# A two-stage token-mixing kernel on one core: its hand-merged generators against recorded tasks that a list scheduler puts in order, with r loaded six tokens to a partition

## Chip, cores, metric

The kernel runs on one core of one Trainium2 chip. The metric is the device time of one execution in microseconds; a median of several runs is given. The profile is that of one execution; for the kernel before it was one of 218.0 us, which is not among the first three below and is 4 us faster than their median. The span, which the profile page states, is about 2 us shorter than the time of the same execution.

The engines are called as the profile calls them: PE is TensorE (PEld its weight loads), DVE is VectorE, ACT is ScalarE, POOL is GpSimd, SP is SyncE, which here only issues transfers.

## The reference

```python
# r, k, v: (4, 8, 768, 48) = batch, head, token, dim; w, u: (8, 48)
for t in range(S):                       # stage 1: a linear attention with decay w
    kt, vt, rt = k[:, :, t], v[:, :, t], r[:, :, t]
    cur   = einsum('bhd,bhe->bhde', u * kt, vt)
    y[:, :, t] = einsum('bhd,bhde->bhe', rt, state + cur)
    state = w * state + einsum('bhd,bhe->bhde', kt, vt)
x = y.transpose(0, 2, 1, 3).reshape(B, S, 384)
theta  = x @ w_theta                     # stage 2: mixing over tokens and channels
zr, zi = x * cos(theta), x * sin(theta)
uu = x + w_tok_r @ zr + w_tok_i @ zi     # 768 x 768 weights, over tokens
out = uu + relu(uu @ w_ch)
```

Both kernels do stage 1 in blocks of 128 tokens. r and k are scaled by powers of w, transposed on PE, evicted to SBUF, multiplied (scores), masked, and applied to v; a running state Y carries what lies before the block. Call stage 1 and the computation of theta, cos and sin of one batch its *front*, and the rest its *mixing*.

## The kernel before

Each stage is a Python generator, and a merge function draws from mixing(b) and front(b+1) in turn. Within what is drawn, the framework's own scheduler orders the instructions. PSUM is cut into three pools of 2, 3 and 3 banks. The pieces that matter here are these (cuts are marked):

```python
loads = ctx.enter_context(tc.tile_pool(name="loads", bufs=7))
for src, nm, eng in ((k, "k_f", nc.scalar), (r, "r_f", nc.sync), (v, "v_f", nc.sync)):
    ts = [loads.tile([C, H, D], F32, name=nm) for c in range(CPH)]
    for c in range(CPH):                         # 128 tokens x 8 heads x 192 bytes each
        eng.dma_start(out=ts[c],
            in_=src[b, :, t0 + c*C : t0 + (c+1)*C, :].transpose([1, 0, 2]))
# ... cut: front, for one block of 128 tokens
p = transposes([Rw ... x4] + [Kw ... x4])        # 8 transposes into one PSUM tile
nc.scalar.activation(RKT.rearrange("p a h t -> p (a h) t"), p, Act.Copy)   # 1024 wide, contiguous
# ... cut: scores, mask, outputs; after the whole of Y:
nc.scalar.activation(Sb[q, :, hp, hi*D:(hi+1)*D], Y[q, :, hp, :], Act.Copy,
                     scale=wC[q, hp:hp+1])       # 8 of these for a batch
# ... cut
merge((mixing(b), 18), (front(b + 1), 21))
```

## Time and profile before

The median of the first three runs is 222.4 us (221.7 to 224.5).

| view | reading |
|---|---|
| span | 216.3 us |
| busy PE / DVE / ACT / POOL | 151.3 / 127.8 / 110.6 / 75.6 us |
| last zr multiply of batch 0, 1, 2, 3 ends at | 61.5, 115.3, 154.9, 193.1 us |
| DMA queues | 81051 packets, 58.0% of 16 engines' span (sum of the queue shares) |

The third row is read from the timeline of DVE: the zr multiply is the last step of a batch's front, so its end is a milestone, and the differences between milestones are the time of one batch. First come lines of the profile page: busy time, then the busy tenths of 40 equal slices of the span (a slice is 5.4 us; PEclk is the clock that TensorE was granted).

```profile
PE 151.3 (70%) x1561; PEld 100.9 (47%) x1561; DVE 127.8 (59%) x268; ACT 110.6 (51%) x194; POOL 75.6 (35%) x89
...
PE   0004696049459689789897987787997778797782
...
ACT  0076363366984468865674351748555173841101
...
PEclk9999999999985589999999999999999999999997
DMA  5999999999999969278502001020200102020122
```

No engine is full as a whole, and the DMA engines are nearly full for the first third. The timeline shows how the kernel starts (start and length in us, engine, line, operation):

```profile
3.22 8.63 ACTq L74 DMA_DIRECT2D k_f<-in_k_dram  x5
...
11.88 1.28 ACT L110 ACT_TABLE_LOAD   x1 [11.88 <-DMA k_f<-in_k_dram]
...
15.86 0.60 ACT L114 ACTIVATE wpinv<-lw_f,niota_p 128x384 f32<-128x384 f32 x1
```

ACT is busy issuing loads until 11.9 us and only then computes the powers of w. In a steady batch (a window of 38.3 us; each engine's busy time and its number of instructions, then clock, DMA share, GB/s) PE works 31.1 us:

```profile
core 0: us, PE busy (x) PEld busy (x) DVE busy (x) ACT busy (x) POOL busy (x), PEclk, DMA share, GB/s
116.70:155.00 38.30, 31.13 (x371) 20.58 (x369) 26.97 (x59) 20.93 (x35) 15.66 (x17) 1.00 0.09 32
```

Finally the costliest ACT group and one of the state scalings (count, busy us, mean ns of one, idle time before it).

```profile
L203 ACT ACTIVATE RKT<-tp 128x1024 bf16<-128x1024 bf16 x24 | 24.1, 1023 | 16.6 <-PE tp L154 14.0 <-DMA wsq_f<-in_moe_w_theta_dram 1.5 <-PE mm L237 1.0
...
L254 ACT ACTIVATE Sblk_172<-Y,wC 64x240 bf16<-64x240 f32 x16 | 7.9, 492 | 4.6 <-DVE Y L247 4.4
```

### The profile page before, as it was taken

Reading aid. Unit: us, or ns where it says so; the run is one execution under the profiler, and the core shown is the slowest. Engines: PE = TensorE matmul, PEld = TensorE weight load, DVE = VectorE, ACT = ScalarE, POOL = GpSimd, SP = SyncE. Lnnn points to the kernel's source line nnn. Section 1 sums busy time; section 2 is a strip of 40 time slices with the busy share of each in tenths; the row PEclk is TensorE's granted clock in tenths of the full one; section 3 lists DMA queues with packets and bytes.
Section 4 is the critical chain, followed back from the end, with each engine's and each line's share of the span. In section 5 each row is a group of like instructions: output and inputs, shape, how many; then the busy total and the mean of one; then the engine's idle time right before and its main releaser. Section 6 shows DMA issues by size and latency. Waiting matters only on the chain.

```text
span 216.3 us, 4058 instructions
## 1 busy us (share of the span) xinstructions
PE 151.3 (70%) x1561; PEld 100.9 (47%) x1561; DVE 127.8 (59%) x268; ACT 110.6 (51%) x194; POOL 75.6 (35%) x89
## 2 busy tenths in 40 slices
PE   0004696049459689789897987787997778797782
PEld 0003475036237466665554555564554556444450
DVE  1009988525676785366656899445698944643231
ACT  0076363366984468865674351748555173841101
POOL 8309338241771733102344481306313120630000
PEclk9999999999985589999999999999999999999997
DMA  5999999999999969278502001020200102020122
GB/s 120 188 187 263 269 211 200 238 190 176 191 198 226 257 168 282 74 146 184 144 2 77 0 20 57 3 73 0 76 0 14 62 0 76 2 73 17 59 73 73
DMA packets 81051, 25.23 MB, mean 117 GB/s; under 512 B 75528, under 2 KB 79496, under 8 KB 81032
## 3 DMA queue, kind: packets, MB, share of 16 engines
q1 hardware_dynamic: 54784, 17.31, 39.1%
q10 hardware_dynamic: 26248, 7.67, 18.4%
q8 instruction: 12, 0.20, 0.4%
q14 instruction: 7, 0.06, 0.1%
HBM read 20.25 MB, written 4.72 MB: 115 GB/s over the span
## 4 chain that ended last, share of the span: by engine, by line
PE 43%; ACT 24%; DMA 16%; DVE 12%; issue 3%; ACTq 1%; SPq 0%
PE mm L322 9%; PE mm L319 9%; DMA k_f<-in_k_dram 7%; PE tp L154 6%; DMA v_f<-in_v_dram 6%; ACT RKT L203 5%; PE mm L331 5%; PE at L212 3%; PE mm L297 3%; ACT uT L286 3%; ACT Sblk_172 L254 3%; PE tp L173 3%; DMA r_f<-in_r_dram 3%; DVE prodT L207 3%; ACT Sblk_170 L254 3%
## 5 line engine op out<-in xcount | busy, mean ns | idle before, releaser
L261 POOL TENSOR_TENSOR ydiag<-dg,vb 128x384 bf16<-128x384 f32 x24 | 21.3, 903 | 42.6 <-DVE x_n L277 23.9
L303 POOL TENSOR_TENSOR zi<-x_n,sinv 128x384 bf16<-128x384 bf16 x24 | 22.4, 945 | 38.4 <-ACT sinv L301 36.0
L203 ACT ACTIVATE RKT<-tp 128x1024 bf16<-128x1024 bf16 x24 | 24.1, 1023 | 16.6 <-PE tp L154 14.0
L218 DVE TENSOR_TENSOR mAT<-at,mask_131 128x512 bf16<-128x512 f32 x48 | 31.1, 682 | 2.1 <-PE at L212 1.8
L319 PE MATMUL mm<-zr,WrT 128*128 128x384 bf16 x144 | 29.1, 326 | 2.9 <-DVE Y L247 1.7
L322 PE MATMUL mm<-zi,WiT 128*128 128x384 bf16 x144 | 28.0, 326 | 0.0
L304 DVE TENSOR_TENSOR zr<-x_n,cosv 128x384 bf16<-128x384 bf16 x24 | 17.5, 733 | 13.0 <-ACT cosv L302 13.0
L324 DVE TENSOR_TENSOR u_n<-x_n,mm 128x384 bf16<-128x384 bf16 x24 | 13.3, 552 | 19.0 <-PE mm L322 18.8
L196 POOL TENSOR_TENSOR Rw_158<-r_f,wpow 128x384 bf16<-128x384 f32 x12 | 12.9, 1081 | 24.6 <-PE tp L154 9.0
L212 PE MATMUL at<-RKT 64*128 64x128 bf16 x192 | 16.0, 250 | 7.0 <-ACT RKT L203 6.5
L334 DVE SCALAR_TENSOR_TENSOR fin<-mm,u_n 128x384 f32<-128x384 f32 x24 | 13.1, 554 | 12.7 <-PE mm L331 12.7
L331 PE MATMUL mm<-Wch,uT 128*128 128x384 bf16 x72 | 15.2, 327 | 7.5 <-ACT uT L286 7.5
L286 ACT ACTIVATE uT<-tp 128x768 bf16<-128x768 bf16 x12 | 9.8, 815 | 18.2 <-PE tp L154 18.0
L322 PEld LDWEIGHTS <-WiT 128*128 128x128 bf16 x144 | 13.9, 98 | 10.1 <-issue 1.2
L297 PE MATMUL mm<-Wth,xT 128*128 128x384 bf16 x72 | 15.5, 344 | 4.4 <-ACT xT L286 4.0
L319 PEld LDWEIGHTS <-WrT 128*128 128x128 bf16 x144 | 13.5, 97 | 10.4 <-DVE Y L247 2.1
L277 DVE TENSOR_TENSOR x_n<-mm,ydiag 128x384 bf16<-128x384 f32 x24 | 12.8, 551 | 8.3 <-PE mm L273 8.2
L207 DVE TENSOR_TENSOR prodT<-RKT 128x512 bf16<-128x512 bf16 x24 | 13.5, 564 | 6.8 <-ACT RKT L203 6.7
L196 POOL TENSOR_TENSOR Rw_162<-r_f,wpow 128x384 bf16<-128x384 f32 x12 | 12.8, 1074 | 11.2 <-DMA r_f<-in_r_dram 5.1
L286 ACT ACTIVATE xT<-tp 128x768 bf16<-128x768 bf16 x12 | 9.5, 818 | 13.3 <-PE tp L154 13.3
L301 ACT ACTIVATE sinv<-mm 128x384 bf16<-128x384 f32 x24 | 11.8, 493 | 8.7 <-PE mm L297 8.4
L173 PE MATMUL tp<-ident_f,wn 128*128 128x128 f32 x72 | 14.8, 326 | 0.8 <-DMA wn<-in_moe_w_tok_r_dram 0.5
(84 smaller groups left out, 253.7 us busy)
## 6 DMA issues: line engine op xcount, KB each, us to landing
k_f<-in_k_dram ACTq DMA_DIRECT2D x24, 192.0 KB, 4.8
r_f<-in_r_dram SPq DMA_DIRECT2D x24, 192.0 KB, 6.3
v_f<-in_v_dram SPq DMA_DIRECT2D x24, 192.0 KB, 5.2
out_dram<-fin SPq DMA_DIRECT2D x24, 192.0 KB, 1.9
wn<-in_moe_w_tok_i_dram ACTq DMA_DIRECT2D x6, 384.0 KB, 4.8
wn<-in_moe_w_tok_r_dram SPq DMA_DIRECT2D x6, 384.0 KB, 4.6
wsq_f<-in_moe_w_theta_dram ACTq DMA_DIRECT2D x1, 576.0 KB, 7.9
wsq_f<-in_moe_w_ch_dram SPq DMA_DIRECT2D x1, 576.0 KB, 7.7
```

The source lines that it names most:

```text
L173: nc.tensor.matmul(p[:, j, :], wn[:, 3 * sg + j, :], ident_f, is_transpose=True, start=(j == 0), stop=(j == 2))
L196: nc.gpsimd.tensor_mul(Rw[:, c, :, :D], r_f[c], wpow)
L203: nc.scalar.activation(RKT.rearrange("p a h t -> p (a h) t"), p, Act.Copy)
L212: nc.tensor.matmul(ats[hi][:, hp, :], RKT[q, 1, hp, :], RKT[q, 0, hp, :], start=(hp == 0), stop=(hp == HP - 1))
L218: nc.vector.tensor_mul(mAT[:, hi], ats[hi], mask_bc)
L261: nc.gpsimd.tensor_mul(ydiag, dataclasses.replace(dgc, ap=list(dgc.ap) + [[0, D]]), vb[:, cc])
L286: nc.scalar.activation(dst.rearrange("p t d c -> p (t d) c"), p, Act.Copy)
L297: nc.tensor.matmul(th_p, xT[:, to % 2, dk, :], Wth[:, dk, :], start=(dk == 0), stop=(dk == ND - 1))
L303: nc.gpsimd.tensor_mul(zi[:, to, :], x_n[:, to, :], sinv)
L319: nc.tensor.matmul(y_p, WrT[:, so, to * C:(to + 1) * C], zr[:, so, :], start=(so == 0), stop=False)
L322: nc.tensor.matmul(y_p, WiT[:, so, to * C:(to + 1) * C], zi[:, so, :], start=False, stop=(so == NCH - 1))
L331: nc.tensor.matmul(f_p, uT[:, to % 2, dk, :], Wch[:, dk, :], start=(dk == 0), stop=(dk == ND - 1))
```

## The change

The intent is a better order on every in-order engine, and cheaper loads. All work is recorded first as tasks, each with an engine, an estimated duration in ns, what it reads and writes, and a priority. A list scheduler then plays the tasks forward in time, at each moment starting the ready task of best priority on each free engine, and hands out eight PSUM banks from one pool. The instructions are emitted in that order.

```diff
+class Plan:
+    def add(self, eng, ns, fn, rd=(), wr=(), prio=0.0, lat=60.0, acq=(), use=(), mode=None): ...
+    def order(self):                      # cut to its core
+        for e in waiting:
+            while free_at[e] <= now:
+                best = # the ready task of lowest (prio, seq) whose PSUM banks are free
+                free_at[e] = now + best.ns
+                best.end = now + best.ns + best.lat
+                out.append(best)
+
+    def act_ns(n, psum=True):
+        return n / 1.2 + (60 if psum else 95)
+
+    def load_r(b):                        # six tokens, 1152 bytes, to a partition
+        P.add(SP, 3200, lambda: nc.sync.dma_start(
+            out=t, in_=r[b].rearrange("h (p n) d -> p h (n d)", n=NCH)), ...)
+
+    def flip6(dst, blocks, tok, prio, rd, wr):
+        P.add(PE, 55 * n, go, ..., acq=[tok])            # n transposes into a bank
+        P.add(ACT, act_ns(n * C), lambda: nc.scalar.activation(
+            dst, bank16(tok)[:, :n * C].rearrange("p (a c) -> p a c", a=n), Act.Copy), ...)
+
+        # r: token 6p + n stands in partition p, so its transposes come out n by n,
+        # and the eviction puts them back in the order of tokens
+        flip6(RT[:, hp].rearrange("q (p n) -> q n p", n=NCH),
+              [Rw[:, n, 2*hp:2*hp+2, :] for n in range(NCH)], ...)
...
-    merge((front(0, *cur), 21))
+    front(0, 0); token_weights(20); square(moe_w_ch, Wch, "Wch", 40)
+    for b in range(B):
+        if b + 1 < B: front(b + 1, 100 * (b + 1))
+        mixing(b, 100 * b + 150)
+    for t in P.order(): t.fn()
```

Smaller parts that come with it: all large loads are issued by SP, the state is scaled on POOL block by block instead of on ACT at the end, cos goes back to PSUM and is read from there, and k, v and the diagonal term are handled two blocks at a time.

## The prediction

> **What bounds it now.** Span 216.3 us; median of three runs 222.4. No engine is full (busy: PE 151.3, DVE 127.8, ACT 110.6, POOL 75.6 us); the limit differs by stage.
>
> 1. *0 to 62 us, batch 0's front alone: loads and order of issue.* The 40-slice row shows DMA 90% busy from 3% to 38% of the span. Solving queue 1 against queue 10 in the queue table gives an estimate of 21 ns per 192-byte packet and 40 us per MB per engine for long rows; k, r, v are 73728 such packets, about 97 us of 16 engines. The Trainium skill's "DMA: Bandwidth & Descriptors" (Specifications) names 512 B as the smallest transfer for line rate; this estimate (9 against 25 GB/s per engine) agrees. In the timeline ACT issues loads until 11.9 us before its first table load, so wpinv ends at 16.5; the chain then waits 12.8 us for v, which stands behind r.
> 2. *62 to 100 us:* the chain holds two more k loads (5.2, 5.0 us); PE clock 0.77 over 50 to 75.
> 3. *Steady batches (116.7 to 155 us, 38.3 each):* PE 31.1, DVE 27.0, ACT 20.9, POOL 15.7 busy. PE, 81% busy, waits in program order behind short chains (RKT eviction, eight Sblk scalings of 0.49 us, flips).
> 4. *Tail from 191 us:* PE stops about 2 us per pair for u_n, flip, eviction.
>
> **What changes.**
> - r becomes 4096 packets of 1152 B: 32 down to 12 us of DMA (estimate). Batch 0's r, k, v and w_theta need about 22 us, then come the token weights, then r of batch 1 at about 40 us.
> - Loads leave ACT: six wpow instead of one add 3 us, yet wpinv is ready at about 11 us, 5 earlier.
> - Sblk scaling (15.8 us of ACT) becomes 20 small POOL products, which don't wait for the whole Y. 160 N=48 matmuls replace 80 N=96: +2.4 us PE.
> - Paired prodT, and zr reading cos from PSUM, save some 6 us of DVE.
> - PE interleaves mixing(b) with front(b+1), three matmuls at a time, through eight shared banks. PE work: 4 x 31 + 12 (token-weight transposes) + 2.4, about 139 us at full clock.
>
> **On the critical path.** Front 0 should end near 42 us instead of 62 (DVE needs about 25 us for it, from 11 us on, with waits). By then PE has done about 20 of 139 us. The other 119 at 88% busy (81% before) take 135: span 42 + 135 + 3 for the last eviction and store = 180. Of the gain (estimates): start 15 to 20, batches 1 to 3 about 15, tail 3 to 4.
>
> **Prediction: 181 us**, 169 to 195 in 8 of 10 cases. Faster by over 2%: 0.96; within 2%: 0.03; slower: 0.01.
>
> **What would show it.** Last zr multiply of batch 0 at 40 to 45 us (62 before); DMA at 0.9 until only 35 to 45 us, its total down about 20 us of 16 engines; no chain piece over 3 us for r or v after 25 us; PE 85 to 90% busy from 60 us to the tail, clock near 1; tail gaps under 1 us except after the last pair; ACT busy near 100, DVE 115 to 122 us.
>
> **What would make it wrong.** The scheduler's durations for POOL and strided DVE forms are guesses: engines run in order, so a piece placed too early blocks everything behind it, and steady batches stay at 38 us (span near 190). Strided writes (RT at a step of 6, x by half heads) or four-dimensional POOL products may be slow; DVE, at 27 to 30 us per batch, is then the limit. All loads and stores share one queue; stores that wait for DVE may hold later loads back.

## The result

The changed kernel takes 206.55 us (205.5 to 207.6, four runs), against 222.2 for the kernel before. The ratio is 0.928 (95% interval 0.920 to 0.936). A ratio here is the mean time of one kernel's fast runs over that of the other's in the same rounds, so it is not quite the ratio of the medians. The direction was right; the size was not. 41 us were forecast and about 16 came, and 206.5 lies outside the stated range of 169 to 195.

The same lines of the page, after (a slice is now 5.1 us):

```profile
PE 145.3 (71%) x1641; PEld 95.7 (47%) x1641; DVE 124.6 (61%) x260; ACT 123.3 (60%) x165; POOL 75.1 (37%) x73
...
PE   0008178896582897599933988999329989999971
...
ACT  2299987999599706409999433755992327511120
...
PEclk9999999999669589969995899999985999999998
DMA  4999209999899992829290510022020002022222
```

ACT is the engine that grew, from 110.6 to 123.3 us, though the state scaling (15.8 us) left it. PE does nearly the same work and still has deep holes: among them slices 21 and 22 and slices 29 and 30, counted from 1 (102 to 112 and 143 to 153 us), and in both places ACT stands at 9. The DMA row has a hole in the slices at about 20 to 31 us and stays high until about 75 us, where 35 to 45 was forecast.

Milestones (end of the last zr multiply of each batch, in us) show where the time went:

| kernel | batch 0 | batch 1 | batch 2 | batch 3 | span |
|---|---|---|---|---|---|
| before | 61.5 | 115.3 | 154.9 | 193.1 | 216.3 |
| after | 59.9 | 99.5 | 136.7 | 176.7 | 204.4 |
| forecast | 42 | | | | 180 |

The lines behind batch 0's entries, the last zr multiply before and after (start and length):

```profile
60.62 0.92 DVE L304 TENSOR_TENSOR zr<-x_n,cosv 128x384 bf16<-128x384 bf16 x1 [0.15 <-ACT cosv L302]
```

```profile
59.33 0.55 DVE L562 TENSOR_TENSOR zr_128<-bank_65,x_125 128x384 bf16<-128x384 f32 x1
```

Batch 1 became 14 us shorter, but this is partly work that moved: the 72 transposes of the token weights on PE ran from 54.0 to 92.3 us before, mostly in batch 1, and run from 30.7 to 47.5 us now, inside batch 0. The steady batches 2 and 3 take 37.1 and 40.1 us, against 39.6 and 38.3 before: they gained nothing. The groups by form show the reason for ACT's growth. These are the evictions of transposed r, one line for each PSUM bank (count, busy us, mean ns of one):

```profile
L382 ACT ACTIVATE RT_104<-bank_65 128x768 bf16<-128x768 bf16 x2 | 5.7, 2844 | 0.4 <-PE bank_65 L379 0.4
L382 ACT ACTIVATE RT_104<-bank_63 128x768 bf16<-128x768 bf16 x2 | 5.9, 2946 | 0.0
L382 ACT ACTIVATE RT_105<-bank_66 128x768 bf16<-128x768 bf16 x2 | 5.7, 2842 | 0.1
```

An eviction of 768 columns takes 2.84 to 2.95 us where one of 1024 took 1.02. It is the one that writes at a step of six elements (12 bytes). The scheduler counts it as 768/1.2 + 60 = 700 ns. The timeline of ACT in batch 2 shows what that does:

```profile
99.31 2.78 ACT L382 ACTIVATE RT_104<-bank_65 128x768 bf16<-128x768 bf16 x1 [0.45 <-PE bank_65 L379]
101.70 2.98 ACT L382 ACTIVATE RT_104<-bank_66 128x768 bf16<-128x768 bf16 x1
104.29 2.95 ACT L382 ACTIVATE RT_104<-bank_61 128x768 bf16<-128x768 bf16 x1
106.85 2.94 ACT L382 ACTIVATE RT_104<-bank_63 128x768 bf16<-128x768 bf16 x1
109.40 1.03 ACT L382 ACTIVATE uT_138<-bank_64 128x768 bf16<-128x768 bf16 x1
110.31 1.02 ACT L382 ACTIVATE KT_106<-bank_62 128x1024 bf16<-128x1024 bf16 x1
```

The starts are about 2.56 us apart, although each record is about 2.95 long. The Trainium skill ("Perfetto Trace Analysis", Per-instruction lifecycle) says that an ACT record ends with the acknowledged write, and that the next instruction may begin its prefetch before that. The overlap of the records agrees, so 2.56 us is taken as the occupancy, and the scheduler is wrong by a factor of 3.7. Behind the four stands uT, which belongs to the mixing of the batch before, and on PE the matmuls that need it, with nothing put ahead of them for the last 5.3 us:

```profile
104.73 0.43 PE L479 MATMUL bank_66<-vb_101,Kw_98 128*64 128x48 bf16 x16 [0.71 <-ACT RT_104 L382]
110.48 1.14 PE L604 MATMUL bank_68<-Wch,uT_138 128*128 128x384 bf16 x3 [5.32 <-ACT uT_138 L382]
```

The windows around these evictions, in batches 2 and 3 (same columns as before), have ACT full and PE at 41% busy:

```profile
99.30:111.00 11.70, 4.78 (x80) 3.73 (x79) 6.35 (x12) 11.69 (x6) 8.47 (x7) 0.84 0.65 118
140.40:153.00 12.60, 5.15 (x93) 4.22 (x93) 3.32 (x9) 12.58 (x7) 1.01 (x2) 0.94 0.16 62
```

The chain that ended last runs through the same instructions in batch 0, through the small loads of w and u at the start, and through the load of r for batch 1:

```profile
2.52 6.10 DMA wu<-in_u_dram
...
15.66 5.76 ACT RT_104 L382 x3
...
41.09 10.45 DMA r_f_93<-in_r_dram
```

### The profile page after: what moved, and what is told of

It is laid out like the page before. It is cut to its first block, busy times and chain, and to the rows that moved or that the text cites. A ratio compares the mean times of both kernels' runs of the same rounds, so it can differ in the third digit from the quotient of the medians.

```text
span 204.4 us, 4137 instructions
## 1 busy us (share of the span) xinstructions
PE 145.3 (71%) x1641; PEld 95.7 (47%) x1641; DVE 124.6 (61%) x260; ACT 123.3 (60%) x165; POOL 75.1 (37%) x73
## 2 busy tenths in 40 slices
DMA packets 60092, 25.25 MB, mean 124 GB/s; under 512 B 50472, under 2 KB 58536, under 8 KB 60072
## 4 chain that ended last, share of the span: by engine, by line
PE 41%; ACT 21%; DVE 19%; issue 8%; DMA 8%; POOL 1%; ACTq 0%; POOLq 0%; DVEq 0%; SPq 0%
ACT RT_104 L382 8%; ACT RT_105 L382 7%; DMA r_f_93<-in_r_dram 5%; PE bank_66 L586 5%; PE bank_64 L586 3%; DMA wu<-in_u_dram 3%; PE bank_68 L586 2%; PE bank_63 L586 2%; PE bank_65 L586 2%; DVE Y_116 L494 2%; DVE mAT_114 L443 2%; ACT wpow L297 2%; PE bank_67 L586 1%; PE bank_62 L586 1%; DVE Kw_96 L416 1%
## 5 line engine op out<-in xcount | busy, mean ns | idle before, releaser
L499 POOL TENSOR_TENSOR Sb_118<-Y_116,wC 128x192 bf16<-128x192 f32 x10 | 5.4, 544 | 34.0 <-DVE Y_116 L494 18.6
L586 PEld LDWEIGHTS <-WiT 128*128 128x128 bf16 x144 | 12.8, 98 | 6.8 <-issue 0.5
L397 POOL TENSOR_TENSOR Rw_94<-r_f_92,wpow 128x576 bf16<-128x576 f32 x6 | 10.1, 1713 | 10.1 <-ACT wpow L297 10.1
L397 POOL TENSOR_TENSOR Rw_94<-r_f_93,wpow 128x576 bf16<-128x576 f32 x8 | 12.6, 1600 | 0.4 <-DMA r_f_93<-in_r_dram 0.4
L499 POOL TENSOR_TENSOR Sb_117<-Y_116,wC 128x192 bf16<-128x192 f32 x10 | 6.1, 606 | 16.6 <-DVE Y_116 L494 13.5
L379 PEld LDWEIGHTS <-Rw_94 128*128 128x128 bf16 x96 | 8.0, 120 | 8.6 <-issue 6.2
L438 PEld LDWEIGHTS <-KT_107 64*128 64x128 bf16 x96 | 4.1, 116 | 12.4 <-issue 8.1
L449 DVE TENSOR_TENSOR PD_109<-RT_105,KT_107 128x1024 bf16<-128x1024 bf16 x4 | 3.3, 823 | 10.8 <-ACT RT_105 L382 6.6
L449 DVE TENSOR_TENSOR PD_108<-RT_104,KT_106 128x1024 bf16<-128x1024 bf16 x4 | 4.1, 1030 | 6.8 <-ACT KT_106 L382 6.8
L382 ACT ACTIVATE xT_135<-bank_65 128x768 bf16<-128x768 bf16 x2 | 1.6, 810 | 11.0 <-PE bank_65 L379 11.0
L438 PEld LDWEIGHTS <-KT_106 64*128 64x128 bf16 x96 | 3.8, 117 | 8.6 <-ACT KT_106 L382 5.9
L604 PEld LDWEIGHTS <-uT_138 128*128 128x128 bf16 x36 | 3.5, 108 | 8.9 <-ACT uT_138 L382 6.4
L604 PEld LDWEIGHTS <-uT_139 128*128 128x128 bf16 x36 | 3.2, 98 | 7.0 <-ACT uT_139 L382 5.3
L382 ACT ACTIVATE RT_104<-bank_65 128x768 bf16<-128x768 bf16 x2 | 5.7, 2844 | 0.4 <-PE bank_65 L379 0.4
L382 ACT ACTIVATE RT_104<-bank_63 128x768 bf16<-128x768 bf16 x2 | 5.9, 2946 | 0.0
L382 ACT ACTIVATE RT_105<-bank_66 128x768 bf16<-128x768 bf16 x2 | 5.7, 2842 | 0.1
L604 PE MATMUL bank_68<-Wch,uT_138 128*128 128x384 bf16 x6 | 1.8, 424 | 5.3 <-ACT uT_138 L382 5.3
L379 PE MATMUL bank_62<-ident,Rw_94 128*128 128x128 bf16 x12 | 1.3, 261 | 5.8 <-DVE Rw_94 L397 5.8
L552 PEld LDWEIGHTS <-xT_134 128*128 128x128 bf16 x36 | 3.5, 106 | 4.1 <-ACT xT_134 L382 2.0
L438 PE MATMUL bank_61<-RT_104,KT_106 64*128 64x128 bf16 x12 | 1.4, 246 | 5.6 <-ACT KT_106 L382 5.6
```

The costliest lines, as they stand in the source:

```text
L379: nc.tensor.matmul(bank16(tok)[:, i * C:(i + 1) * C], s, ident, is_transpose=True, start=(i == 0), stop=(i == n - 1))
L382: P.add(ACT, act_ns(n * C), lambda: nc.scalar.activation(dst, bank16(tok)[:, :n * C].rearrange("p (a c) -> p a c", a=n), Act.Copy), use=[t ...
L397: eng.tensor_mul(Rw[:, :, 2 * hp:2 * hp + 2, :D].transpose([0, 2, 1, 3]), rf[:, 2 * hp:2 * hp + 2, :].rearrange("p h (n d) -> p h n d", n= ...
L438: nc.tensor.matmul(bank(tk[hi])[:, hp * C:(hp + 1) * C], KT[q, c, hp, :], RT[q, hp, cc * C:(cc + 1) * C], start=(hp == 0), stop=(hp == HP ...
L449: nc.vector.tensor_mul(PD, RT[:, :, 2 * pr * C:(2 * pr + 2) * C].rearrange("p h (a t) -> p a h t", a=2), KT)
L499: P.add(POOL, pool_ns(HP * D), lambda cc=cc: nc.gpsimd.tensor_mul(Sb[:, cc], Y[:, cc], wide(wC, D)), rd=[("Y", cc), "wC"], wr=[("Sb", b % ...
```

## The experiments

Theories at the start. **A**: the stepped eviction costs what the prediction missed. **B**: the scheduler's order with its other wrong durations, and the single load queue, cost it. All experiments edit the changed kernel. Times are medians of all runs; ratios are against the kernel before, in the same rounds. e1 to e4 ran on one chip, e5 to e8 on a second, e9 to e11 on a third, e12 on a fourth, so costs are best compared by ratios; 0.01 is about 2.2 us. For e9 to e12 the verdict on record is "unclear", although the intervals all lie below 0.95; in their rounds many executions of the kernel before were slow (3 of 7, and 8 of 12 for e12).

| run | us | ratio, 95% interval |
|---|---|---|
| changed kernel | 206.6 | 0.928 (0.920 to 0.936) |
| e1_flat_wrong | 180.6 | 0.825 (0.820 to 0.829) |
| e2_psum_step | 181.1 | 0.825 (0.820 to 0.831) |
| e3_r_blocks | 182.9 | 0.827 (0.820 to 0.835) |
| e4_true_ns | 186.9 | 0.855 (0.848 to 0.861) |
| e5_flat_told_slow | 186.3 | 0.841 (0.836 to 0.847) |
| e6_theta_own | 207.4 | 0.938 (0.933 to 0.943) |
| e7_wu_first | 178.7 | 0.809 (0.805 to 0.813) |
| e8_told_all | 179.9 | 0.814 (0.808 to 0.819) |
| e9_told_late | 206.6 | 0.932 (0.924 to 0.941) |
| e10_told_all_wu | 176.9 | 0.798 (0.791 to 0.804) |
| e11_tokw_late | 173.1 | 0.782 (0.774 to 0.790) |
| e12_best_r_blocks | 177.4 | 0.812 (0.807 to 0.818) |

### e1_flat_wrong: the eviction contiguous, everything else in place

```diff
-            flip6(RT[:, hp].rearrange("q (p n) -> q n p", n=NCH),
+            flip6(RT[:, hp].rearrange("q (n p) -> q n p", n=NCH),
```

The exponents of w are those of the block layout (one constant changed), to keep the numbers in range. The tokens of r are permuted, so the result is wrong (relative error 1.33).

> Same instructions, same order, same loads as the changed kernel; only the four evictions of the transposed r per batch write their 768 elements next to each other instead of at a step of 6, so the tokens stand in the wrong order and the result is wrong on purpose (r's exponents are those of the block layout, to keep the numbers in range). Theory A (the step in the eviction's write costs ScalarE about 2 us each, 16 times, and holds everything behind it): evictions 0.8 us instead of 2.8 to 3.0, ACT busy about 90 us instead of 123, time 178 to 188 us. Rival B (the order that the list scheduler made, with its other wrong durations, and the one load queue cost the missing 25 us): evictions shorter, but time 198 us or more.

Measured: 180.6 us, eviction 0.81 us (median), ACT busy 94.7 us. With the step in the write go 26 us by the medians, and 0.103 of the time before, about 23 us, by the ratios. A check of the traces shows the same order of instructions on every engine as in the changed kernel, here and in e2; in e3 too, but for the load queue. B as stated falls: the same order, loads and queue give 180.6 when only the eviction is contiguous.

### e2_psum_step: a correct form, with the step on the read from PSUM

```diff
-            dst, bank16(tok)[:, :n * C].rearrange("p (a c) -> p a c", a=n), Act.Copy),
+            dst, bank16(tok)[:, :n * C].rearrange(
+                "p (a c) -> p c a" if swap else "p (a c) -> p a c", a=n), Act.Copy),
-            flip6(RT[:, hp].rearrange("q (p n) -> q n p", n=NCH), ...)
+            flip6(RT[:, hp].rearrange("q (p n) -> q p n", n=NCH), ..., swap=True)
```

> A correct form: the same eviction writes SBUF contiguously, and reads PSUM at a step of 128 elements with 6 as the inner count, so the step moves from the write to the read. Theory A with the cost in the write: eviction 0.8 to 1.0 us, time 178 to 190 us. If a stepped read of 2-byte elements from PSUM costs the same, the eviction stays at 2.5 us or more and the time at 203 to 209. Rival B: 198 us or more whatever the eviction takes.

Measured: 181.1 us, correct. The view by tile gives duration (min/median/max in ns) of the evictions; first e2, then, for comparison, e4 below, which keeps the step on the write:

```profile
L382 ACT ACTIVATE RT<-bank x16: 804/811/842, 15.8 to 127.4; 128x768 bf16<-128x768 bf16 x16
```

```profile
L382 ACT ACTIVATE RT<-bank x16: 2736/2916/3097, 15.9 to 137.0; 128x768 bf16<-128x768 bf16 x16
```

The same 768 two-byte elements in another order: a step of 256 bytes on the read costs ACT nothing (0.811 us), a step of 12 bytes on the write costs 2.1 us. Why the write is slow, no run shows. With this edit the steady batches take 31.2 and 31.4 us. PE is 87% busy in the first and 95% in the second, and 95% in a window that covers parts of both:

```profile
115.00:150.00 35.00, 33.30 (x417) 21.52 (x415) 27.51 (x63) 19.14 (x34) 13.83 (x12) 1.00 0.13 47
```

### e3_r_blocks: undo the load half of the change

```diff
-        P.add(SP, 3200, lambda: nc.sync.dma_start(
-            out=t, in_=r[b].rearrange("h (p n) d -> p h (n d)", n=NCH)), ...)
+        def go():
+            for n in range(NCH):
+                nc.sync.dma_start(out=t[:, :, n * D:(n + 1) * D],
+                                  in_=r[b, :, n * C:(n + 1) * C, :].transpose([1, 0, 2]))
+        P.add(SP, 3200, go, ...)
```

with the eviction contiguous and the exponents of the block layout.

> Undo the load part alone: r comes in as six blocks of 128 tokens (192-byte packets again, 81 thousand packets instead of 60), the eviction is then contiguous and the result correct; the scheduler and the shared banks stay. Theory A: evictions 0.8 us, DMA busy up by about 20 us of 16 engines as an estimate, time 183 to 195 us, faster than the changed kernel. Rival B: no faster than the changed kernel, 204 us or more, since it adds DMA time to the one queue.

Measured: correct, ratio 0.827, the same as e2 within its interval, although 80892 packets (not 60092) put about 17 us of 16 engines' time back (68.6% of 180.1 us against 59.2% of 179.7). Batch 0's milestone is later than in e2 (58.0 against 54.5 us), and batch 1 makes it up. So the change without the wide load (the scheduler and the smaller parts) gives the whole of e2's gain, and the wide load of r, as it came, cost about 22 us (0.101) through its eviction and saved none that shows here.

### e4_true_ns: the step stays, the scheduler is told

```diff
-        P.add(ACT, act_ns(n * C), lambda: nc.scalar.activation(
+        P.add(ACT, ns or act_ns(n * C), lambda: nc.scalar.activation(
-              ("TR", b, hp), base + hp, [("Rw", hp)], [("RT", b % 2, hp)])
+              ("TR", b, hp), base + hp, [("Rw", hp)], [("RT", b % 2, hp)], ns=2560)
```

> The stepped eviction stays, but the scheduler is told its measured start-to-start time (2560 ns instead of 700), so only the order of instructions changes. Theory A: the work is still there, time 198 to 208 us. Rival B in the form that the wrong duration only spoilt the order: 192 us or less.

Measured: 186.9 us. A said 198 or more, because the work is still there, and it is: ACT is busy 122.6 us and each eviction takes 2.92. So A as I stated it falls. B as stated at the start had fallen with e1, but the form of it written for this run, that the wrong duration only spoilt the order, said 192 or less, and that is met. Telling the truth won back 0.073, about 16 us. It came after batch 0's front: the milestone of batch 0 is no earlier than in the changed kernel (62.2 against 59.9 us). The granted clock is not the reason, since it was 0.928 in the profiled execution of e4 and 0.921 in that of the changed kernel. In the windows of the r evictions of batches 2 and 3 ACT is as full as in the changed kernel, but PE is 81 to 84% busy:

```profile
95.50:108.00 12.50, 10.14 (x114) 6.56 (x111) 8.88 (x26) 12.50 (x8) 7.53 (x8) 1.00 0.15 55
126.50:141.00 14.50, 12.11 (x129) 7.77 (x128) 6.38 (x24) 14.48 (x12) 4.09 (x6) 0.88 0.15 56
```

ACT and PE in batch 2 show how. The uT eviction now stands after the first of the four, and PE has mixing matmuls to do while the rest are evicted:

```profile
95.54 2.74 ACT L382 ACTIVATE RT<-bank 128x768 bf16<-128x768 bf16 x1
97.90 1.01 ACT L382 ACTIVATE uT<-bank 128x768 bf16<-128x768 bf16 x1
98.81 7.92 ACT L382 ACTIVATE RT<-bank 128x768 bf16<-128x768 bf16 x3
```

```profile
98.97 1.15 PE L605 MATMUL bank<-Wch,uT 128*128 128x384 bf16 x6 [0.21 <-ACT uT L382]
...
101.65 2.12 PE L587 MATMUL bank<-zr,WrT 128*128 128x384 bf16 x12
103.61 2.11 PE L587 MATMUL bank<-zi,WiT 128*128 128x384 bf16 x12
```

The count of 384-column matmuls that stand on PE between the first transpose of r and the first score of a batch, from the order of instructions, says the same. At about 0.16 us each, 12 of them fill 2 us and 45 fill 7:

| kernel | batch 1 | batch 2 | batch 3 |
|---|---|---|---|
| changed kernel, e2 (told 0.70 us) | 12 | 12 | 9 |
| e4, e5 (told 2.56 us) | 24 | 45 | 45 |
| e9 (told 0.70 us, result 7.5 us late) | 42 | 51 | 42 |

The new theory is **C**: the loss comes from the order that a wrong duration made.

### e5_flat_told_slow: the fourth cell

```diff
-        P.add(ACT, act_ns(n * C), lambda: nc.scalar.activation(
+        P.add(ACT, 2560 if swap else act_ns(n * C), lambda: nc.scalar.activation(
```

on top of e2.

> The fourth cell of work by told duration: the eviction is the cheap one of e2_psum_step (0.81 us), but the scheduler is told 2560 ns, as in e4_true_ns. Theory C (the loss of 25 us is mostly the order made from a wrong duration, and the 33 us of extra ScalarE work cost only some 6 us once planned for): a duration told too long spoils little, because an engine that is done early only waits; 180 to 188 us, about the cheap and well-told 181. Rival D (any wrong number in the plan costs as much, in either direction): 195 us or more. If the order of e4_true_ns is just a luckier order whatever the eviction costs: below 179 us.

Measured: 186.3 us. That completes a table of work by told duration (ratios to the kernel before):

| | told 0.70 us | told 2.56 us |
|---|---|---|
| eviction takes 0.81 us | 0.825 (e2) | 0.841 (e5) |
| eviction takes 2.9 us | 0.928 (changed kernel) | 0.855 (e4) |

The traces of e4 and e5 show one order of instructions, as those of e2 and the changed kernel do, so each column compares the work alone. Read by columns, the extra ACT work (16 evictions, whose records are 2.1 us longer each; ACT's busy time grows by 28 us, since the records overlap, and not by the 33 that the expectation says) cost 0.103 of the time before, about 23 us, when the plan does not know it, and 0.013, about 3 us, when it does. The 3 is rough, for the intervals of e4 and e5 are each 0.006 wide to either side. Read along the rows, a duration told too long costs 0.016, one told too short 0.073. D, which expected both directions to be alike, falls. C expected 180 to 188 and about 181; the careful order costs some 3.5 us by itself (0.016), so C was somewhat optimistic.

### e6_theta_own: is it the stop of the load queue?

```diff
+            own = sb.tile([C, n * HD], F32, name=f"th{o}") if late else None
-            i = load_rows(s3[:, o:o + n], n, late)
+            i = load_rows(s3[:, o:o + n], n, late, own)   # staged in a tile of its own
```

The order of instructions is identical to the changed kernel's on every engine.

> The changed kernel with its stepped eviction and exactly its order of instructions on every engine; only the two staging tiles of w_theta are tiles of their own, so that the load queue no longer stands from about 19 to 29 us behind the w_theta casts, which wait on ScalarE behind four stepped evictions. Theory E (a good part of the loss is this stop of the only load queue, which makes r of batch 1 late, 10.5 us on the chain): the DMA gap at 20 to 29 us closes, r of batch 1 lands 8 us or more earlier, time 195 to 202 us. Theory C without it (ScalarE itself is late in every batch, the loads only follow): 202 to 207 us.

Measured: 207.4 us, no gain. But the edit did only half of what it was to do. The load of v at 19.7 us no longer waits until 29.4, and DMA is full until about 26 us, but the queue then stops at the token weights, and DMA is empty from 31 to 36 us instead. The profile puts the two longest of these waits, 4.5 and 6.2 us, down to ACT: they end when ACT has cast v out of the staging buffers, behind the slow evictions. r of batch 1 is issued when it was before (41.1 us):

```profile
19.71 1.06 SPq L324 DMA_DIRECT2D ld<-in_v_dram  x2
...
28.72 7.01 SPq L334 DMA_DIRECT2D ld<-in_moe_w_tok_i_dram  x2
...
41.12 0.70 SPq L316 DMA_DIRECT2D r_f<-in_r_dram  x1
```

So closing this one gap gains nothing, but what an earlier r of batch 1 would be worth with this order stays open.

### e7_wu_first and e8_told_all: two repairs on e2

e7 issues the two small loads of w and u (1.5 KB each) from SP, ahead of r (the memset before them is also ranked first and told 0 ns):

```diff
-            nc.scalar.dma_start(out=wu[:HP, :, :D], ...); nc.scalar.dma_start(out=wu[HP:, :, :D], ...)
-        P.add(ACT, 200, wu_load, wr=["wu"], prio=-99, lat=3000)
+            nc.sync.dma_start(out=wu[:HP, :, :D], ...); nc.sync.dma_start(out=wu[HP:, :, :D], ...)
+        P.add(SP, 1900, wu_load, wr=["wu"], prio=-3e6, lat=3000)
```

> On top of e2_psum_step: the two small loads of w and u (1.5 KB each) are issued ahead of r on the load queue instead of on ScalarE's queue beside it. In e2 they landed at 8.8 us and held the powers of w until 10.9. Theory: they land at about 5 us, the powers start at about 7, r lands 2 us later but before it is needed, the first scores 2 to 4 us earlier; time 176 to 180 us. If the loads and not the powers pace batch 0, 180 to 182 us.

Measured: 178.7 us. The powers of w start at 6.0 us instead of 10.9, and batch 0's milestone moves from 54.5 to 52.7:

```profile
4.48 0.20 ACT L288 ACTIVATE lw_p<-wup 128x4 f32<-128x4 f32 x1
...
6.00 3.14 ACT L297 ACTIVATE wpow<-lw_f,tok_f 128x384 f32<-128x384 f32 x6
```

e8 changes nine told durations and nothing else (four shown):

```diff
-                P.add(DVE, 270 if cc == 0 else 480, update, ...)
+                P.add(DVE, 270 if cc == 0 else 700, update, ...)
-                P.add(DVE, dve_ns(HD), lambda c=c, Kw=Kw, ik=ik: ...)      # 475
+                P.add(DVE, 850, lambda c=c, Kw=Kw, ik=ik: ...)
-            P.add(..., dve_ns(576) if on_dve else pool_ns(576), scale_r, ...) # 675, 1313
+            P.add(..., 1300 if on_dve else 1600, scale_r, ...)
-                P.add(PE, 330, scores, ...)
+                P.add(PE, 430, scores, ...)
```

> On top of e2_psum_step, only the order changes: nine durations of the plan are set to start-to-start times read from the traces (state update 0.70 instead of 0.48 us, k scaling 0.85 instead of 0.48, r scaling on GpSimd 1.6 instead of 1.3, and six smaller ones). Theory C says that only a duration that is too short by some microseconds in a row does harm, and these are off by under 0.4 us each: 177 to 184 us. Rival D: 174 us or less.

Measured: 179.9 us, ratio 0.814 against e2's 0.825: about 1% for errors of at most 0.63 us each. (The expectation says under 0.4 us each; for r scaling on DVE it is 0.63.) The size is as C expected.

### e9_told_late: which order matters, TensorE's or ScalarE's?

```diff
-            use=[tok], wr=wr, prio=prio)
+            use=[tok], wr=wr, prio=prio, lat=lat)       # lat=7500.0 for r, 60 otherwise
```

> The changed kernel with its stepped eviction; the scheduler still believes that the eviction takes ScalarE 0.7 us, but that its result comes 7.5 us late, which is about when the last of four in a row is really done. So TensorE's order knows when the scores can start (36 to 45 matmuls of 384 columns then stand between the last transposes of r and the first scores in each batch, 6 in the changed kernel), ScalarE's order does not know that it is busy. Theory F (the loss is TensorE standing in order before the scores with too little put ahead of them): 184 to 193 us. Rival G (the loss is ScalarE's order, four evictions in a row with other evictions stuck behind them): 200 us or more.

(The expectation counts from the last transpose: 6 in the changed kernel, 36 to 45 here.)

Measured: 206.6 us, as slow as the changed kernel, so F falls as it was stated: filling PE was not enough. The waits name why (total us, times, longest):

```profile
PE bank L480 <- ACT vb L425: 12.8, 3, 7.3
```

PE had its 42 to 51 matmuls of 384 columns, but many stood behind the state's outer products, which need v from ACT, and ACT did v behind the slow evictions. The scheduler knew that r comes late; it did not know that ACT is occupied, so everything else that comes from ACT was placed too early. That agrees with G, though a run that changes ACT's order alone was not made. The run also changes one thing more: the scheduler frees a PSUM bank only when the result that is read from it counts as done, so the late result keeps four of the eight banks out of the plan for 7.5 us each. What that did to the order was not measured.

### e10_told_all_wu and e11_tokw_late

e10 is e7 and e8 together. e11 also ranks the token-weight transposes behind batch 0's front:

```diff
-    token_weights(20)
+    token_weights(36)
```

> e7_wu_first and e8_told_all together. If the two gains add: 176 to 178 us; if the new order takes the start's gain back: 178 to 181.

> e10_told_all_wu with the transposes of the token weights ranked behind all of batch 0's front (priority 36 instead of 20), so that the last pair of batch 0 is not held by transposes whose rows have not landed (5.9 us on the chain of e2_psum_step). Theory: batch 0's last zr multiply at 48 us or earlier (54.5 in e2), time 171 to 176 us. If the transposes are then merely in the way of batch 1: 176 to 181 us.

Measured: 176.9 and 173.1 us. The two repairs add up. In e11 batch 0's milestone comes at 48.6 us (56.1 in e10; 48 or earlier was expected), and PE's granted clock over the profiled run is 0.98, against 0.92 in the changed kernel. e11 is correct and beats both kernels: 22% under the kernel before and about 16% under the changed one.

### e12_best_r_blocks: the wide load of r again, in the best version

The edit is that of e3 on top of e11, told 6300 ns.

> e11_tokw_late, but with r loaded in six blocks of 128 tokens again, told as 6300 ns instead of 3200. It asks whether the load half of the change is worth anything once the order is good: 20 us more DMA time of 16 engines as an estimate. If DMA paces batch 0 in this version: 176 us or more (ratio 0.79 or more, against 0.782 of e11_tokw_late). If it does not: 172 to 175 us.

Measured: 177.4 us, ratio 0.812 (0.807 to 0.818) against 0.782 (0.774 to 0.790). That is in the band for "DMA paces batch 0", but batch 0 is not where the time went, so that theory is not shown. The version with the wide load is about 3% faster here, with 60092 packets instead of 80892, whereas in e3 the wide load was worth nothing. The two ran on different chips, and telling another load time also changes the order, so the 3% holds for the two versions and not for the load's own time. Their batch 0 milestones are 49.1 and 48.6 us; the difference came later, between 86.6 and 146.2 us (86.4 and 142.9 in e11).

## Why the prediction was right or wrong

- **What bounds the kernel before** held: loads and their issue at the start, then PE behind short chains, then a tail with stops.
- **The failed step is the sum under "On the critical path": both of its terms lacked the wait for ACT at the r evictions.** "Front 0 should end near 42 us" measured 59.9. "The other 119 at 88% busy (81% before) take 135", 138 with its last 3 us, measured 144.5 (204.4 minus 59.9): PE was 78% busy there, and 41% around the r evictions of two batches. The prediction kept these evictions at the cost of contiguous ones ("ACT busy near 100"); ACT was busy 123.3, and 95.1 in e2. With the cheap eviction in the same order (e2) the terms are 54.5 and 125.2, so about 5 us of the loss lay in the first and 19 in the second.
- **It had named the risk and mis-sized it.** The stepped write of RT stands in its last list without a number, and the risk of poor durations was put on POOL and DVE, when the wrong one was on ACT. What it wrote there, "a piece placed too early blocks everything behind it, and steady batches stay at 38 us", is what came (37.1 and 40.1 us), though the span was 204.4 and not "near 190".
- **The mechanism of the loss is the work under an order that does not know it** (e1, e2, e4, e5): the extra ACT work costs about 3 us under the order made from 2.56 us and about 23 under the one made from 0.70.
- **"Front 0 should end near 42 us" was wrong by itself too**: 54.5 us even with the cheap eviction. wpinv was ready at 14.4 us and not at about 11, because the small loads of w and u landed at 8.6 us beside r; e7, which mended that, moved the milestone by 1.8 us. And the prediction had PE do about 20 us of its work by then; in e2 all the token-weight transposes ran inside front 0, and PE had done 32.4 us. e11, which ranks them lower, took 7.5 us off this milestone, though they still ran from 24.7 to 45.3 us. e11 ends it at 48.6; the remaining 6 us are not explained.
- **The second term would have held at 88%.** In e2 PE is 87% busy after batch 0's front. That term is then 125.2 us and not 138, because more of PE's work had been done before it. So the late first term and the short second one are in part the same work, moved, and their sum, a span of 179.7, comes close to the forecast 180 by luck. That agreement is no success of the sum.
- **DMA** fell from 58.0% of 216.3 us to 51.0% of 204.4 (queue shares times span), from 125 to 104 us of 16 engines. The forecast of about 20 us is met. The traffic still did not end at 35 to 45 us, since the queue stops for buffers, and a piece of 10.5 us for r lies on the chain where none over 3 was forecast. The time saved paid nothing in e2 against e3, and about 3% in e11 against e12, with the limits said there.
- **The tail** came as forecast: in the chain, PE matmuls follow each other from 189 us to the last pair.

## What to carry to other kernels

A list scheduler in the kernel depends on its durations, and here an error was not symmetric: one op told 3.7 times too short and run four in a row cost 0.073 of the time, and the same op told about as much too long cost 0.016. So run once, read start-to-start times of every group from the trace, and put them back before judging the idea. When a layout change makes a transfer cheaper, follow the data to the instruction that has to undo the layout, and put the step on the side that does not pay for it (here the read from PSUM).

## What the Trainium skill lacked or had wrong

- "SBUF — State Buffer" (the note on cachelines) says that SBUF has 16-byte lines and that one can stride for free up to 8 bf16 elements. Here ScalarE's write of 768 bf16 elements at a step of 6 took 2.92 us (median) and 0.81 when contiguous; the starts were 2.56 us apart. That step was not free for this write. The same note also asks for at least two hits per line, which steps of 12 bytes do not give on every line, so its two halves point different ways here; no run separates them.
- No page that was read gives the price of a ScalarE read of PSUM at a step. A read of bf16 at a step of 128 elements, six at a time, cost nothing: 0.811 us, the same as contiguous.
- "DMA: Bandwidth & Descriptors" (Issuing engines are not separate DMA queues) says that the time a sequencer takes to issue a DMA is usually small relative to the DMA. In the kernel before, five loads of k (192 KB each, a median of 4.8 us from issue to landing) kept ACT's queue for 8.6 us, 1.7 us each, and its first computation until 11.9 us; in the changed kernel the first two loads of k took SP 3.5 us, and later pairs from 1.1 us up. On an engine that also computes that is not small.
- The same page (Specifications) names 512 B as the smallest transfer for line rate. That agrees with the estimate from the queues of the kernel before, 21 ns per 192-byte packet, and with the fall of 21 us when r came in 1152-byte packets; no run tried sizes near 512 B.
